# A delta-rule attention with two expert layers: two buffers for r's second layout, whole-row moves of y, each unit's second product reordered, and the weights' low word multiplied on DVE

## The chip, the cores and the metric

One core of a Trainium2 chip runs the whole program. The metric is the device time of one execution in microseconds (us); lower is better. PE is the matmul engine (PEld its weight loads), DVE, ACT and POOL are the vector, scalar and GpSimd engines, and SP is the engine whose queue issues all the DMAs of this kernel.

## The reference

Three stages follow each other. Every array of the attention has 4 batches, 8 heads, 768 steps and 40 channels; the 3072 tokens have 320 features.

```python
# attention, per batch and head, state 40x40
for t in range(768):
    y[t] = r[t] @ state
    Sa = state @ a[t]
    state = state * w[t] - outer(Sa, b[t]) + outer(v[t], k[t])
# first expert layer: one expert, d_ff 2048; its weights come as float64
x = relu(x @ w_in) ** 2 @ w_out
# second expert layer: four experts, d_ff 1024, mixed by normalised probabilities
out = sum(p[:, e:e + 1] * (relu(x @ w1[e]) @ w2[e]) for e in range(4))
```

## The kernel before

**Tiling.** The time axis is cut into 12 chunks of 64, and each chunk into two steps `s` (24 steps, `attention`), one for each half of the batches (`hb`). Two consecutive steps make one block `k` of 256 tokens (12 blocks). Within a chunk the recurrence is solved in closed form: scans and reciprocals of the decay on DVE (L371, L391), scaling on POOL (L395, L403), products on PE, and a triangular inverse (`invert`, one for each block) of 31 rounds of a multiplication and a subtraction on DVE (L691, L694). The recurrence between chunks runs through `f_mm` (L507), which reads the state and `rf`, a second layout of r that `load_rf` (L337) brings in with a DMA of its own. The tile `rf` has one buffer: the planner's line L357 lets the load of one step start when `f` of the step before has read it.

**From attention to the first layer.** `ys_y` (L632, POOL) leaves a block's output in the tile `y`, as [128, half, head, time]. `to_x1` (L807) turns it into the features-by-tokens tile `xr` with 12 DMAs of 40, 24 or 8 rows each; in `y`, one row of one head is four pieces of 64 numbers that don't lie side by side. `split` takes `xr` apart into a high part `xh` (L818, ACT) and the rest `xl` (L821, DVE), so that PE can multiply in its rounded fp32 format with the accuracy of fp32.

**First expert layer.** A block has 16 units (`moe1_l1`, `moe1_sq`, `moe1_l2`). A unit is 8 matmuls of 256 columns (`ffn1`, L197); ReLU (L753), square (L755) and the rounded copy `gh` (L758) on ACT; the remainder `gl` on POOL (L761); and `ffn2`, 6 matmuls of 320 columns into two accumulators in the order gh, gh, gl for the first and gh, gh, gl for the second (L202 to L204).

**Weights.** The first expert layer's weights come as float64 in 48 slices (`weights`). For each slice ACT takes the absolute value of the high word (L249) and scales the low word by 2^-52 (L250); DVE clamps, shifts, sets the sign and cuts out the power of two (L252, L253, L255, L257); POOL multiplies the low word by that power (L259); ACT rounds (L233); PE adds up the remainder (L237, L239, L240); ACT stores it (L243, L245).

**Second expert layer.** After the last block, 384 units of the same two functions run with nothing else on PE. Each unit's `ffn2` stands one unit behind its `ffn1`.

**What sets the order.** All work up to the units of the last block is entered in a planner, `Schedule`, with an engine, a due time (`DUE`, `LEAD`), the operations it depends on, a planned duration, and the buffers it needs. `run` simulates the engines and writes each engine's instructions in the order that comes out, the SP queue's too; at run time each engine takes its instructions in that fixed order. `PORT` (L62, used at L101 and L120) names operations of DVE and POOL that the simulation does not let overlap. The planned durations are constants in the calls of `op`; a wrong one changes the order and nothing else.

Of the kernel before, what the change touches and what calls it, by code (L numbers as in the profile page):

```python
# [29 lines left out]

E_MIN = 2.0 ** -15
# [9 lines left out]
DUE = dict(block=59.25, step=[-2.0, 3.5, -2.5, 0.3, 0.0], invert=[5.4, -11.9, -40.2], ffn=-2.4, w=[-85.9, 2.32], on_pe=48)  # L41
# [6 lines left out]
class Schedule:  # L48
# [13 lines left out]
    PORT = dict(DVE=("P", "t", "x1l"), POOL=("sq", "scale_a", "kb", "yq", "yf", "w_mul", "w_add"))  # L62
# [74 lines left out]
def tile_delta_rule_moe(  # L137
# [76 lines left out]
    def weights(n, t0):  # L214
# [4 lines left out]
        on_pe = n < DUE["on_pe"]  # L219
# [15 lines left out]
        def rest():  # L235
            v["pw"] = ps1.tile([128, 256], F32, tag="l1", name=f"pw{n}")[:, 0:k]
            pe.matmul(v["pw"], ident, v["m"], start=True, stop=False)  # L237
            if on_pe:
                pe.matmul(v["pw"], ident, v["f"], start=False, stop=False)  # L239
            pe.matmul(v["pw"], idneg, wt[i][:, c0:c1], start=False, stop=True)  # L240

        def low():
# [7 lines left out]
        op(o("w_lo"), "ACT", lambda: act.mul(v["lo"], v["li"], 2.0 ** -52), t0, [o("w_ld")], 0.29)  # L250
# [8 lines left out]
        op(o("w_mul"), "POOL", lambda: pool.tensor_tensor(v["f"], v["lo"], v["f"], ALU.mult),  # L259
           t0 + 2, [o("w_pow"), o("w_lo")] + [("tt", 0)] * (n >= 12), 0.65)  # L260
        if not on_pe:
            op(o("w_add"), "POOL", lambda: pool.tensor_tensor(v["m"], v["m"], v["f"], ALU.add), t0 + 2, [o("w_mul")], 0.65)
        op(o("w_hi"), "ACT", hi, t0 + 2, [o("w_sign" if on_pe else "w_add"), ("w_hi", n - 1)], 0.27)
        op(o("w_pe"), "PE", rest, t0 + 3, [o("w_hi"), o("w_mul")], 0.98 if on_pe else 0.55, alloc=[("l1", 2, [o("w_low")])])
# [25 lines left out]
    def attention(s, tt):  # L290
# [44 lines left out]
        def load_rf():  # L335
            d["rf"] = ap1.tile([128, 4, 128], F32, tag="rf", name=f"rf{s}")
# [20 lines left out]
        op(o("ld_rf"), "SP", load_rf, tt - LEAD["ld_xv"], [], prev=("ld_rf", s - 1), lat=2.7, alloc=[("rf", 1, [o("f")])])  # L357
# [172 lines left out]
        for h in range(2):  # L530
            for j in range(2):
                op(o("a_xv", h, j), "ACT", lambda h=h, j=j: a_xv(h, j), tt - LEAD["vm"], [o("ld_xv"), o("scale_a")], 0.29)
                op(o("s_xv", h, j), "ACT", lambda h=h, j=j: s_xv(h, j), tt - LEAD["f"], [o("ld_xv"), ("yf", s - 2, h)], 0.22)
# [4 lines left out]
        for h in range(2):  # L538
            for j in range(2):
                op(o("vmm", h, j), "DVE", lambda h=h, j=j: vm_mask(h, j), tt - LEAD["vm"] + h, [o("vm"), o("ld_xv")], 0.6)  # L540
# [3 lines left out]
            for j in range(2):  # L544
                op(o("fx", h, j), "ACT", lambda h=h, j=j: f_xv(h, j), tt - LEAD["f"] + h, [o("f"), o("ld_xv")], 0.26)
# [4 lines left out]
            op(o("xc", h), "ACT", lambda h=h: x_copy(h), tt - LEAD["x"] + h, [o("x", h)], 0.4)  # L550
# [31 lines left out]
        for i in range(2):  # L582
            op(o("mt", i), "DVE", lambda i=i: merge1(i), tt - LEAD["merge"], td_in + txo, 0.34)
        op(o("merge1", 1), "PE", lambda: merge1(2), tt - LEAD["merge"], td_in + both("mc") + [("merge1", s - 1, 1)], 0.68,
           alloc=at_bank("", ("y2",)) + [("y2", 1, [o("merge2")])])
        op(o("y2"), "ACT", lambda: merge1(3), tt - LEAD["merge"], [o("merge1", 1)], 0.53)
        op(o("merge2"), "PE", lambda: merge2(0), tt - LEAD["merge"] + 2, td_in + [o("y2")], 0.68, alloc=at_bank("", ("t2",)))
        op(o("t2"), "ACT", lambda: merge2(1), tt - LEAD["merge"] + 2, [o("merge2")], 0.53)
# [55 lines left out]
        for h in range(2):  # L644
# [7 lines left out]
            if not last:  # L652
# [5 lines left out]
               alloc=[] if hb + h else [("y", 1, [("tx1", k, i) for i in range(12)])])  # L658
# [414 lines left out]
```

## Time and profile before

| what | us |
|---|---|
| median of three runs | 1611.57 (1609.05 to 1613.45) |
| the profiled execution, its own time | 1609.46 |
| its span, first to last instruction | 1607.7 |
| PE busy in the span | 1444.4 (90%) |
| DVE, ACT, POOL busy | 835.0, 752.1, 379.6 |

The span is 1.8 us under the execution's own time, and that execution is 2.1 us under the median. PE's share alone doesn't say where time can be had: attention and the first expert layer fill the span up to about 865 us, the last block's units that up to 897 us, and the second expert layer the rest.

### The profile page before, as it was taken

What the parts mean: (1) busy time and instruction counts of PE and PEld (TensorE: products, weight loads), DVE (VectorE), ACT (ScalarE), POOL (GpSimd) and SP (SyncE); (2) the same over time, 40 slices, a digit from 0 to 9 for tenths busy, and PEclk for the clock granted to TensorE, in tenths of its full rate; (3) what the DMA queues carried; (4) which work ended last, traced back from release to release, by engine and by line L of the source; (5) the groups of instructions that cost most, each with busy time, mean ns of one, the idle gap of its engine ahead of it and who ended that gap; (6) DMA issues with size and microseconds to landing.
All of it is one profiled execution on the core that took longest, in us unless ns stands there. A gap on an engine that the chain in (4) does not pass through costs nothing.

```text
span 1607.7 us, 39782 instructions
## 1 busy us (share of the span) xinstructions
PE 1444.4 (90%) x16336; PEld 1354.8 (84%) x16336; DVE 835.0 (52%) x1944; ACT 752.1 (47%) x1991; POOL 379.6 (24%) x539
## 2 busy tenths in 40 slices
PE   5487989889779798887988999999999999999999
PEld 4366777878668687776888999999999999999998
DVE  8888767685675857759542233323333333332332
ACT  6477676566565656656666433322222222222221
POOL 5345443443324343343324200000000000000000
PEclk9798999999899898999999999999999999999999
DMA  7454243342333423243214111100000000000000
GB/s 235 117 144 144 68 126 76 105 122 56 110 73 103 118 56 110 65 117 92 61 32 125 46 50 46 56 1 28 28 19 1 19 10 1 1 7 20 26 26 25
DMA packets 147733, 107.18 MB, mean 67 GB/s; under 512 B 114400, under 2 KB 122080, under 8 KB 147552
## 3 DMA queue, kind: packets, MB, share of 16 engines
q1 hardware_dynamic: 147552, 104.64, 23.2%
q8 instruction: 129, 2.11, 0.5%
q14 instruction: 52, 0.43, 0.1%
HBM read 85.34 MB, written 14.55 MB: 62 GB/s over the span
## 4 chain that ended last, share of the span: by engine, by line
PE 48%; SPq 1%; DVE 1%; DMA 1%; ACT 0%; issue 0%; POOL 0%; DVEq 0%; ACTq 0%
PE z L197 22%; PE pz L204 7%; PE pz L202 7%; PE pz L203 7%; PE h L197 2%; SPq L807 1%; PE py L204 1%; PE py L202 0%; PE ptr L922 0%; PE py L203 0%; DVE xv L601 0%; DMA mu<-md 0%; PE pys L609 0%; DMA td<-mu 0%; PE ptx L597 0%
## 5 line engine op out<-in xcount | busy, mean ns | idle before, releaser
L969 DVE SCALAR_TENSOR_TENSOR zl<-z,zh 128x256 fp32r<-128x256 f32 x384 | 163.0, 425 | 476.4 <-ACT zh L968 476.4
L968 ACT ACTIVATE zh<-z 128x256 fp32r<-128x256 f32 x384 | 147.1, 383 | 510.5 <-PE z L197 510.5
L197 PE MATMUL z<-x2h,w 128*128 128x256 f32 x1920 | 380.8, 282 | 0.0
L197 PE MATMUL z<-x2l,w 128*128 128x256 f32 x1152 | 320.4, 278 | 0.0
L197 PEld LDWEIGHTS z<-x2h,w 128*128 128x128 f32 x1920 | 306.2, 188 | 0.0
L203 PE MATMUL pz<-w,zh 128*128 128x320 f32 x768 | 237.3, 309 | 0.0
L204 PE MATMUL pz<-w,zl 128*128 128x320 f32 x768 | 237.0, 309 | 0.0
L202 PE MATMUL pz<-w,zh 128*128 128x320 f32 x768 | 236.8, 308 | 0.0
L761 POOL TENSOR_TENSOR gl<-r,gh 128x256 fp32r<-128x256 f32 x192 | 144.7, 755 | 320.6 <-ACT gh L758 251.3
L197 PE MATMUL h<-xh,w 128*128 128x256 f32 x960 | 213.2, 304 | 6.2 <-ACT xh L818 6.1
L197 PEld LDWEIGHTS z<-x2l,w 128*128 128x128 f32 x1152 | 216.8, 188 | 0.0
L197 PEld LDWEIGHTS h<-xh,w 128*128 128x128 f32 x960 | 168.6, 206 | 11.3 <-ACT xh L818 6.8
L197 PE MATMUL h<-xl,w 128*128 128x256 f32 x576 | 171.9, 299 | 1.6 <-DVE xl L821 1.6
L691 DVE TENSOR_TENSOR tmp<-mu,t 128x126 f32<-128x126 f32 (+22 forms) x372 | 128.9, 347 | 46.7 <-DMA mu<-md 35.3
L753 ACT ACTIVATE r<-h 128x256 f32<-128x256 f32 x192 | 73.4, 382 | 153.6 <-PE h L197 130.4
L204 PEld LDWEIGHTS pz<-w,zl 128*128 128x128 f32 x768 | 144.3, 188 | 0.1
L202 PEld LDWEIGHTS pz<-w,zh 128*128 128x128 f32 x768 | 144.3, 188 | 0.0
L203 PEld LDWEIGHTS pz<-w,zh 128*128 128x128 f32 x768 | 144.2, 188 | 0.0
L204 PE MATMUL py<-w,gl 128*128 128x320 f32 x384 | 125.8, 328 | 19.1 <-POOL gl L761 17.9
L202 PE MATMUL py<-w,gh 128*128 128x320 f32 x384 | 128.0, 333 | 9.5 <-ACT gh L758 9.1
L185 POOL TENSOR_TENSOR w<-raw,w 64x128 fp32r<-64x128 f32 x32 | 31.6, 988 | 441.5 <-ACT w L183 405.9
L694 DVE TENSOR_TENSOR t<-t,tmp 128x126 f32<-128x126 f32 (+22 forms) x372 | 123.0, 331 | 9.0
(105 smaller groups left out, 2491.4 us busy)
## 6 DMA issues: line engine op xcount, KB each, us to landing
in<-kba SPq DMA_DIRECT2D x24, 768.0 KB
raw<-wf SPq DMA_DIRECT2D x32, 352.0 KB
raw<-wm SPq DMA_DIRECT2D x32, 234.0 KB
wd<-w SPq DMA_DIRECT2D x24, 264.0 KB
r<-rv SPq DMA_DIRECT2D x24, 256.0 KB
v<-rv SPq DMA_DIRECT2D x24, 256.0 KB
rf<-rv SPq DMA_DIRECT2D x24, 256.0 KB
mu<-md SPq DMA_DIRECT2D x24, 256.0 KB
```

The costliest lines, as they stand in the source:

```text
L185: pool.tensor_tensor(t[64:128, 576:704], raw[64:128, 576:704], t[64:128, 576:704].bitcast(F32), ALU.subtract)
L197: pe.matmul(ps, a, b, start=n == 0, stop=n == len(mm) - 1)
L202: pe.matmul(pys[tt], gh[:, sl], t[:, 256:576], start=first, stop=False)
L203: pe.matmul(pys[tt], gh[:, sl], t[:, 960:1280], start=False, stop=False)
L204: pe.matmul(pys[tt], gl[:, sl], t[:, 256:576], start=False, stop=last)
L691: dve.tensor_tensor(v["tmp"], a, b, ALU.mult)
L694: dve.tensor_tensor(c, c, v["tmp"], ALU.subtract)
L753: act.activation(g["r"], g["ps"], AF.Relu)
L761: pool.tensor_tensor(g["gl"], g["r"], g["gh"].bitcast(F32), ALU.subtract)
L807: sp.dma_start(v["raw"][r0:r0 + e1 - e0, kc].rearrange("p (a b x) -> p a b x", a=2, b=2), src)
L968: act.activation(gh, ps, AF.Relu)
L969: dve.scalar_tensor_tensor(gl, ps, 0.0, gh.bitcast(F32), ALU.max, ALU.subtract)
```

## The change

1. `rf` gets two buffers; its load waits for `f` of the step before last.
2. `y` is laid out as [128, head, half and half of the heads, time], so that the four pieces of one head lie side by side, and each of the 12 moves reads one run of 256 numbers in a row.
3. `ffn2` runs the four matmuls with gh first and the two with gl last. In the first expert layer, ACT writes `gh` as the square of the ReLU directly; the unrounded square comes after it, in place.
4. For the weights, ACT's scaling of the low word and POOL's multiplication go; DVE does both in one operation. The condition that held slices from the 13th on back until the first inverse was turned goes with POOL's operation.
5. The planner's `PORT` names DVE's operations of the weights; `w_mul` and `w_add` leave POOL's list. Twelve planned durations are raised (by 0.02 to 0.24). The setting `on_pe` was 48, all slices, so what it chose stays.

```diff
-DUE = dict(block=59.25, ..., w=[-85.9, 2.32], on_pe=48)
+DUE = dict(block=59.25, ..., w=[-85.9, 2.32])
...
-    PORT = dict(DVE=("P", "t", "x1l"), POOL=("sq", "scale_a", "kb", "yq", "yf", "w_mul", "w_add"))
+    PORT = dict(
+        DVE=("P", "t", "x1l", "w_clamp", "w_shift", "w_sign", "w_pow", "w_mul"),
+        POOL=("sq", "scale_a", "kb", "yq", "yf"),
+    )
...
             pe.matmul(pys[tt], gh[:, sl], t[:, 256:576], start=first, stop=False)
             pe.matmul(pys[tt], gh[:, sl], t[:, 960:1280], start=False, stop=False)
+        for tt in range(2):
+            sl = slice(tt * 128, tt * 128 + 128)
             pe.matmul(pys[tt], gl[:, sl], t[:, 256:576], start=False, stop=last)
...
-        op(o("w_lo"), "ACT", lambda: act.mul(v["lo"], v["li"], 2.0 ** -52), t0, [o("w_ld")], 0.29)
...
-        op(o("w_mul"), "POOL", lambda: pool.tensor_tensor(v["f"], v["lo"], v["f"], ALU.mult),
-           t0 + 2, [o("w_pow"), o("w_lo")] + [("tt", 0)] * (n >= 12), 0.65)
+        op(o("w_mul"), "DVE", lambda: dve.scalar_tensor_tensor(
+            v["f"], v["li"], 2.0 ** -52, v["f"], ALU.mult, ALU.mult), t0 + 1, [o("w_pow")], 0.32)
...
-            d["rf"] = ap1.tile([128, 4, 128], F32, tag="rf", name=f"rf{s}")
+            d["rf"] = ap2.tile([128, 4, 128], F32, tag="rf", name=f"rf{s}")
...
-        op(o("ld_rf"), ..., alloc=[("rf", 1, [o("f")])])
+        op(o("ld_rf"), ..., alloc=[("rf", 2, [o("f")])])
...
-                d["y"] = ap1.tile([128, 2, 8, 64], F32, tag="y", name=f"y{s}")
+                d["y"] = ap1.tile([128, 4, 4, 64], F32, tag="y", name=f"y{s}")
-            pool.tensor_tensor(st[2 * k]["y"][:, hb, hs], d["t", h][:, :, 0:64], d["q"][:, hs], ALU.mult)
+            pool.tensor_tensor(st[2 * k]["y"][:, :, 2 * hb + h], d["t", h][:, :, 0:64], d["q"][:, hs], ALU.mult)
...
         elif i == 1:
+            g["gh"] = fp.tile([128, 256], F32R, tag="gh", name=f"gh{k}_{f}", bufs=3)
+            act.activation(g["gh"], g["r"], AF.Square)
+        elif i == 2:
             act.activation(g["r"], g["r"], AF.Square)
-        elif i == 2:
-            g["gh"] = fp.tile([128, 256], F32R, tag="gh", name=f"gh{k}_{f}", bufs=3)
-            act.copy(g["gh"], g["r"])
...
-            src = y[64 * (hd % 2) + e0:64 * (hd % 2) + e1, :, hd // 2::4]
-            sp.dma_start(v["raw"][r0:r0 + e1 - e0, kc].rearrange("p (a b x) -> p a b x", a=2, b=2), src)
+            src = y[64 * (hd % 2) + e0:64 * (hd % 2) + e1, hd // 2].rearrange("q a x -> q (a x)")
+            sp.dma_start(v["raw"][r0:r0 + e1 - e0, kc], src)
```

## Rows read from the trace of the kernel before

**Rows 1.** Busy time by stretch: us, then PE, PEld, DVE, ACT, POOL, granted clock, DMA.
```profile
0.00:132.00 132.00, 78.56 (x1243) 62.36 (x1243) 112.23 (x299) 81.32 (x247) 55.78 (x77) 0.87 0.58 174
...
410.00:480.00 70.00, 58.20 (x888) 51.51 (x888) 45.21 (x105) 42.21 (x111) 25.63 (x38) 0.89 0.36 92
...
897.00:1607.70 710.70, 706.78 (x5446) 706.40 (x5444) 225.62 (x502) 185.06 (x456) 25.05 (x25) 1.00 0.07 23
```
**Rows 2.** PE in order of time near 475 us: start, us, operation [idle before <-releaser].
```profile
467.39 0.69 PE L507 MATMUL pf<-rf,SS 64*64 64x64 f32 x32
...
477.35 1.12 PE L493 MATMUL pk<-cs,in 128*128 128x128 f32 x4 [2.08 <-ACT m L440]
481.97 1.32 PE L507 MATMUL pf<-rf,SS 64*64 64x64 f32 x32 [3.51 <-DMA rf<-rv]
```
**Rows 3.** The SP queue in order of time, same stretch.
```profile
467.47 10.67 SPq L807 DMA_DIRECT2D xr<-y  x12
478.24 0.44 SPq L781 DMA_DIRECT2D y1d<-y  x1
478.78 0.36 SPq L337 DMA_DIRECT2D rf<-rv  x1
```
**Rows 4.** DVE in order of time, same stretch.
```profile
480.49 0.96 DVE L821 TENSOR_TENSOR xl<-xr,xh 128x768 fp32r<-128x768 f32 x1 [0.69 <-ACT xh L818]
```
**Rows 5.** Waits up to 865 us: who waited for whom, total us, times, longest.
```profile
PE pf L507 <- DMA rf<-rv: 28.8, 7, 10.6
...
PE py L204 <- POOL gl L761: 17.7, 36, 1.7
...
PE pw L239 <- POOL raw L259: 17.5, 9, 8.1
...
PE h L197 <- ACT xh L818: 6.1, 3, 4.0
```
**Rows 6.** Lines 807, 348 and 818 alone: duration ns min/median/max, first and last start.
```profile
L807 SPq DMA_DIRECT2D xr<-y x144: 721/778/1687, 112.6 to 860.5; - x144
...
L348 SPq DMA_DIRECT2D xv<-vn x24: 533/554/684, 5.0 to 797.1; - x24
...
L818 ACT CAST xh<-xr x12: 831/831/855, 124.5 to 862.8; 128x768 fp32r<-128x768 f32 x12
```
**Rows 7.** The chain that ended last, from 844 us: start, us, what.
```profile
850.05 0.74 POOL y L632
...
851.51 0.84 SPq L807
...
864.72 5.07 PE h L197 x23
...
870.67 0.95 PE h L197 x8
```
**Rows 8.** Lines 252 and 255 alone, as rows 6.
```profile
L252 DVE TENSOR_SCALAR raw<-raw x48: 219/276/1585, 9.4 to 173.6; 128x234 f32<-128x234 f32 x32, 128x236 f32<-128x236 f32 x16
...
L255 DVE SCALAR_TENSOR_TENSOR raw<-raw x48: 333/397/919, 11.6 to 174.5; 128x234 uint32<-128x234 uint32 x32, 128x236 uint32<-128x236 uint32 x16
```
**Rows 9.** Groups by line and shape up to 860 us: busy us, mean ns | idle before.
```profile
L259 POOL TENSOR_TENSOR raw<-raw 128x234 f32<-128x234 f32 x32 | 24.0, 753 | 35.4 <-DVE tmp L691 10.2 <-DVE raw L257 7.1 <-PE pw L240 5.1
...
L252 DVE TENSOR_SCALAR raw<-raw 128x234 f32<-128x234 f32 x32 | 13.9, 434 | 10.8 <-ACT raw L249 10.6
...
L250 ACT ACTIVATE raw<-raw 128x234 f32<-128x234 uint32 x32 | 13.1, 409 | 0.0
```
**Rows 10.** POOL in order of time, 44 to 90 us.
```profile
76.86 2.72 POOL L259 TENSOR_TENSOR raw<-raw 128x236 f32<-128x236 f32 x5
```
**Rows 11.** PE in order of time in the second expert layer, 1200 to 1204 us.
```profile
1201.44 0.31 PE L202 MATMUL pz<-w,zh 128*128 128x320 f32 x1
...
1201.74 0.31 PE L204 MATMUL pz<-w,zl 128*128 128x320 f32 x1
1201.88 0.31 PE L202 MATMUL pz<-w,zh 128*128 128x320 f32 x1
```

More of the change, by code (lines that the diff above doesn't have):

```diff
@@ L28 @@
 C_U, C_NEG, C_ID, C_ONE, C_END = 0, 64, 168, 296, 560
+MOVES = []
+for _kc in range(2):
+    MOVES += [(40 * _i, _kc, 3 * _kc + _i, 0, 40) for _i in range(3)]
+    MOVES.append((120, _kc, 6, 8 * _kc, 8 * _kc + 8))
+for _r in (0, 64):
+    MOVES += [(_r, 2, 6, 16, 40), (_r + 24, 2, 7, 0, 40)]
 E_MIN = 2.0 ** -15
@@ L36, in sub @@
     return AP(base.tensor, base.offset, [list(base.ap[0])] + dims)
-DUE = dict(block=59.25, step=[-2.0, 3.5, -2.5, 0.3, 0.0], invert=[5.4, -11.9, -40.2], ffn=-2.4, w=[-85.9, 2.32], on_pe=48)
+DUE = dict(block=59.25, step=[-2.0, 3.5, -2.5, 0.3, 0.0], invert=[5.4, -11.9, -40.2], ffn=-2.4, w=[-85.9, 2.32])
 LEAD = dict(
@@ L237, in rest @@
             pe.matmul(v["pw"], ident, v["m"], start=True, stop=False)
-            if on_pe:
-                pe.matmul(v["pw"], ident, v["f"], start=False, stop=False)
+            pe.matmul(v["pw"], ident, v["f"], start=False, stop=False)
             pe.matmul(v["pw"], idneg, wt[i][:, c0:c1], start=False, stop=True)
@@ L258, in weights @@
             v["fi"], v["mi"], 0xFF800000, None, ALU.bitwise_and), t0 + 1, [o("w_sign")], 0.19)
-        op(o("w_mul"), "POOL", lambda: pool.tensor_tensor(v["f"], v["lo"], v["f"], ALU.mult),
-           t0 + 2, [o("w_pow"), o("w_lo")] + [("tt", 0)] * (n >= 12), 0.65)
[L261 to L264, printed above, removed]
+        op(o("w_mul"), "DVE", lambda: dve.scalar_tensor_tensor(
+            v["f"], v["li"], 2.0 ** -52, v["f"], ALU.mult, ALU.mult), t0 + 1, [o("w_pow")], 0.32)
+        op(o("w_hi"), "ACT", hi, t0 + 2, [o("w_sign"), ("w_hi", n - 1)], 0.29)
+        op(o("w_pe"), "PE", rest, t0 + 3, [o("w_hi"), o("w_mul")], 0.98, alloc=[("l1", 2, [o("w_low")])])
         op(o("w_low"), "ACT", low, t0 + 4, [o("w_pe")], 0.3)
@@ L544, in attention @@
             for j in range(2):
-                op(o("fx", h, j), "ACT", lambda h=h, j=j: f_xv(h, j), tt - LEAD["f"] + h, [o("f"), o("ld_xv")], 0.26)
+                op(o("fx", h, j), "ACT", lambda h=h, j=j: f_xv(h, j), tt - LEAD["f"] + h, [o("f"), o("ld_xv")], 0.37)
             op(o("fc", h), "ACT", lambda h=h: f_copy(h), tt - LEAD["f"] + h, [o("f"), ("ya", s - 2, h)], 0.26)
@@ L582, in attention @@
         for i in range(2):
-            op(o("mt", i), "DVE", lambda i=i: merge1(i), tt - LEAD["merge"], td_in + txo, 0.34)
+            op(o("mt", i), "DVE", lambda i=i: merge1(i), tt - LEAD["merge"], td_in + txo, 0.45)
         op(o("merge1", 1), "PE", lambda: merge1(2), tt - LEAD["merge"], td_in + both("mc") + [("merge1", s - 1, 1)], 0.68,
            alloc=at_bank("", ("y2",)) + [("y2", 1, [o("merge2")])])
-        op(o("y2"), "ACT", lambda: merge1(3), tt - LEAD["merge"], [o("merge1", 1)], 0.53)
+        op(o("y2"), "ACT", lambda: merge1(3), tt - LEAD["merge"], [o("merge1", 1)], 0.76)
         op(o("merge2"), "PE", lambda: merge2(0), tt - LEAD["merge"] + 2, td_in + [o("y2")], 0.68, alloc=at_bank("", ("t2",)))
-        op(o("t2"), "ACT", lambda: merge2(1), tt - LEAD["merge"] + 2, [o("merge2")], 0.53)
+        op(o("t2"), "ACT", lambda: merge2(1), tt - LEAD["merge"] + 2, [o("merge2")], 0.76)
         def tx_mm():
@@ L657, in attention @@
             op(o("yq", h), "POOL", lambda h=h: ys_y(h), tt - LEAD["yq"] + h, [o("ya", h), o("scale_a")] + ([("yq", 2 * k, 0)] if hb + h else []), 0.69,
-               alloc=[] if hb + h else [("y", 1, [("tx1", k, i) for i in range(12)])])
+               alloc=[] if hb + h else [("y", 1, [("tx1", k, i) for i in range(len(MOVES))])])
         if not last:
@@ L824, in split @@
                     sp.dma_start(dbg[k], v["raw"])
[L826 to L831 removed]
         ys = [("yq", 2 * k + b, h) for b in range(2) for h in range(2)]
         done = [("x1h", k), ("x1l", k)]
[L834 removed]
+        for i in range(len(MOVES)):
             op(("tx1", k, i), "SP", lambda i=i: to_x1(i), tt - LEAD["x1"], ys + ([] if i else [("x1l", k - 1)]), 0.65, prev=("tx1", k, 0) if i else None,
                alloc=[] if i else [("ws", 5, done)])
[L837 removed]
+        moved = [("tx1", k, i) for i in range(len(MOVES))]
         end = [("l1", k, NF1 - 1)]
@@ L1017, in _arrays @@
         vn[:, n, :, 4:] = v[:, 4:, n].transpose(0, 2, 1, 3)
-    hd = [(h, e) for h in (0, 1, 2) for e in range(D)] + [(6, e) for e in range(8)]
-    hd += [(h, e) for h in (3, 4, 5) for e in range(D)] + [(6, e) for e in range(8, 16)]
-    hd += [(6, e) for e in range(16, 40)] + [(7, e) for e in range(D)]
+    hd = [(h, e) for _, _, h, e0, e1 in MOVES[:10] for e in range(e0, e1)]
     feat = np.array([h * D + e for h, e in hd])
```

23 lines of the change are left out of this document (7 added, 16 removed).

## The prediction

> **What bounds the kernel now.** The busy times by stretch come first. From 897 us on, PE is busy for 706.8 of 710.7 us at a granted clock of 1.00 [rows 1]: the second expert layer is a plain queue of matmuls, and only what changes their number or pace changes it. What can be won lies before. In a middle block (410 to 480 us) PE is busy for 58.2 of 70 us and the other engines for 45 or less, at a mean clock of 0.89: no engine is full, and PE, the fullest, loses its time in waits and at the lower clock. In the first 132 us it is DVE that is full, 112.2 of 132.
>
> Next, PE in order of time around the end of a block. It waits 2.08 us for ACT's copy of m, and 3.51 us for the DMA that loads `rf` [rows 2]. The SP queue shows why that DMA is late: the step before freed the one buffer at 468.1 (467.39 + 0.69), but the twelve moves of y began at 467.47 and held the queue for 10.67 us; the load of rf went out at 478.78 [rows 2, 3]. The table of waits puts 28.8 us of PE on this load, in 7 waits. The longest, 10.6, is the kernel's first load; that leaves 18.2 in six later ones [rows 5]. The matmuls behind such a stop run at half pace: the same 32 matmuls take 1.32 us instead of 0.69 [rows 2].
>
> The chain of waits from 844 us shows the moves themselves. In the last block y is ready at 850.8, the twelve issues take until about 861.4, and h begins at 864.72 [rows 7]. Blocks follow each other at (862.8 - 124.5) / 11 = 67.1 us [rows 6].
>
> **The change part by part.**
>
> *Two buffers for rf.* The load now waits for a read that lies a whole step back, so SP can issue it ahead of the twelve moves; nothing new queues behind it. In the block of rows 2, `f` could start at about 478.2, behind pk. Six waits go: **18.2 us**. What is late next: h needs xl, which ends at 480.49 + 0.96 = 481.45 [rows 4], while `f` now ends at 481.97 + 1.32 = 483.29 and h starts there. Alone, then, the two buffers give only 1.8 per block; the rest hangs on the next part.
>
> *Moves of one run per row.* The twelve stay twelve, each with a source of two dimensions instead of four. No row shows a move inside SBUF with such a source. Bounds for one issue: 0.36, a plain load [rows 3], and 0.78, as now [rows 6]; a load with a three-dimensional target takes 0.55 [rows 6]. I take 0.44, the store of a plain SBUF tile [rows 3], since it has the same kind of source. Then 12 x (0.78 - 0.44) = 4.1 us are saved before xh, and xl ends at about 477.4, before `f` would: the 18.2 can be kept. Where PE waits for xh itself, 6.1 us in three blocks, the longest 4.0 [rows 5], the 4.1 covers each wait.
>
> *The clock.* After the stop in rows 2 the 32 matmuls cost 0.63 too much. In the last block 23 matmuls of h took 5.07 us, 0.22 each, against 0.95 / 8 = 0.119 later [rows 7]: that is the lower of the two levels, 1.2 against 2.4 GHz. Two units (16 matmuls) at that pace cost 1.6 us, with the 0.63 some 2.2 per block, 13.4 in six. The wait for m stays, so the clock may still fall: I take half, **6.7**, bounds 0 and 13.4. For the last block likewise half of 5.07 - 23 x 0.119 = 2.3; with the 6.1 that makes **7.3**.
>
> *Order in the second product.* PE waits for gl 36 times, 17.7 us in all [rows 5]. Two more matmuls (0.15 each [rows 11]) now run before the wait, so each shrinks by at most 0.29: 10.6 us in all, fewer where the wait was shorter. ACT still runs three operations before gl, so gl comes no earlier. I take **6**, bounds 0 and 10.6. In the second expert layer gl is never late (3.9 us of idle in 710.7 [rows 1]), so nothing is won there. The order changes accumulator four times a unit instead of twice. A step into another accumulator takes 0.14 (1201.74 to 1201.88), two steps within one 0.30 (1201.44 to 1201.74) [rows 11]: switching costs nothing, and the term is 0. The Trainium skill speaks against this edit: "TensorE: Matmul & The Clock Gate", section "A second HAM failure mode: psum-queue depth-cycling", tells of a kernel that cycled through accumulator banks and whose clock swung between its levels. Here PE already changes banks in every unit and the clock is 1.00 [rows 1]; by that rule the time would be that of the last rival.
>
> *The low word on DVE.* ACT loses 48 operations of 0.41 and POOL 48 of 0.75 [rows 9]; neither is full. DVE gains 48. The nearest shape is L255, two tensor inputs with the same strides: median 0.397 [rows 8], so 48 x 0.397 = 19.1 us in the stretch in which DVE is full. Against that, POOL held DVE up: L252 takes 0.276 in the median, but up to 1.585 [rows 8] and 0.434 in the mean [rows 9], 0.158 x 48 = 7.6 us for this one of four lines. The 19.8 us that DVE idles in the first 132 can hold the remaining 11.5. PE waited 17.5 us for POOL's product [rows 5], and five products that waited for the first inverse ran together at 76.86 [rows 10]; that condition goes. Bounds: a loss of 19.1, if nothing comes back, and a gain of 17.5 + 7.6 = 25.1. The two nearly cancel on DVE; of PE's 17.5 I take a quarter: a gain of **4**.
>
> *The planner.* New durations and the port rewrite every engine's order up to 865 us, which no row shows. One wait like the 2.08 of rows 2 more or less in each of nine later blocks is 19 us either way; I take 0.
>
> **Sum.** 18.2 + 6.7 + 7.3 + 6 + 4 = 42.2. The profiled execution took 1609.5, so 1567.3; the median lies 2.1 above it, so **1569**.
>
> **The rivals.**
>
> *The stop moves instead of going.* If an issue keeps 0.78, h waits for xl: 1.8 per block (483.29 to 481.45), 10.8 in six, with 6 for gl and 4 for the weights 20.8: 1611.6 - 20.8 = 1591. If the new order leaves the rf load behind the moves, the first two terms go and 17.3 remains: 1594. For it: moves of 8 to 40 rows have a shortest of 0.72 and a median of 0.78 [rows 6], so it is not the rows that set the price, and perhaps not the pieces either. Against: the plain store behind them costs 0.44 [rows 3].
>
> *The new order removes more.* PE idles 11.8 us of 70 [rows 1], of which I take away less than half. Another 2.08 in nine blocks: about 1550.
>
> *The weights come too late (the slower side).* Place: the first 180 us. DVE alone now carries five operations a slice, between the 62 of each inverse. If it pushes the weights back, the first blocks' units cannot fill PE's gaps, and they end up behind the attention, where nothing overlaps them. Price: a block's 16 units of 0.95 + 6 x 0.15 = 1.85 us, 29.6 per block of lag. It decides once the lag eats the other terms, 42.2 - 4 = 38.2: from 1.3 blocks on. At two blocks: 1611.6 - 38.2 + 59.2 = 1633. Against it: DVE's busy time in the first 132 us barely grows by the count above.
>
> *The order gives everything back,* the terms eaten by new waits: about 1610.
>
> *The clock falls in the second expert layer.* At 1.2 GHz a unit of 1.85 costs another 1.7 or so (0.22 against 0.119 a matmul). From 38.2 / 1.7 = 23 of 384 units on, the kernel is slower than my forecast by all it had won; at one unit in ten, 1569 + 65 = 1634.
>
> **How the numbers follow.** Forecast 0.58, more removed 0.12, the stop moves 0.17, no change 0.04, late weights 0.08, clock 0.01. A difference of about 0.3% (5 us) is what a measurement of this kernel can tell from none. Faster 0.58 + 0.12 + 0.17 = 0.87, same 0.04, slower 0.09. The range runs from 1543 (the order's 19 and the other half of the clock's 13.4 on top of the forecast) to 1600, which holds the first rival at both its prices with a few us for the weights; what lies above and below is under 2 in 10.
>
> **What would show it.** In the profile after: L807's median near 0.44; the moves of a block under 6 us; the load of rf ahead of them and no wait of PE on it after the first; xh then ready before `f` ends, and the clock in middle blocks above 0.95; the waits for gl fewer or shorter by 0.3; no line for ACT's or POOL's part of the weights, the DVE line near 0.4 and L252's mean nearer its median; the second expert layer still about 711 us. I am wrong if L807 stays near 0.78, if PE waits for xh or for another load in rf's place, if the weights' last L255 starts later than now (174.5 us), or if blocks still follow at over 65 us.

## The result, and the profile after

The changed kernel takes **1570.09 us** in the median of four runs (1568.11 to 1590.19), the kernel before 1611.51 beside it; the ratio is **0.9755, with the interval 0.9716 to 0.9793**. The profiled run took 1568.11, its span is 1566.3, 41.4 less than before. The kernels before that ran beside the experiments on other chips had medians from 1611.5 to 1616.8; so kernels are compared below by their ratios, and by microseconds only within a trace.

The number forecast was 1569. The steps to it were mostly wrong, as the rest of this document shows.

First the busy time by stretch (columns as in [rows 1]): the first stretch, a block in the middle, five blocks from the split of x in the fifth to that in the tenth, and the second expert layer.

```profile
0.00:123.00 123.00, 84.65 (x1221) 66.69 (x1221) 106.83 (x328) 71.70 (x216) 30.75 (x46) 0.83 0.59 169
398.00:460.00 62.00, 53.68 (x888) 48.87 (x888) 46.12 (x104) 41.73 (x111) 25.75 (x38) 0.97 0.37 101
398.25:713.34 315.09, 275.04 (x4440) 248.55 (x4440) 236.05 (x518) 208.12 (x551) 128.58 (x190) 0.96 0.37 100
856.00:1566.30 710.30, 706.14 (x5442) 705.81 (x5440) 225.55 (x502) 184.88 (x456) 25.08 (x25) 1.00 0.07 23
```

The second expert layer is as long as it was, 710.3 against 710.7 us [rows 1]. The same five blocks before:

```profile
410.24:750.35 340.11, 285.11 (x4440) 251.95 (x4440) 227.15 (x515) 209.06 (x550) 129.01 (x190) 0.92 0.35 92
```

They are 25.0 us shorter: PE, with the same 4440 matmuls, is busy for 10.1 us less and idle for 14.9 less (55.0 to 40.1). Up to the second block's split of x 18.3 us are won (215.1 to 196.8), of which 7.0 are left at the third's (279.2 to 272.2); then it is 37.0 up to the tenth's and 40.5 up to the last one's (862.8 to 822.3). Behind that, almost nothing.

Now the end of a block, on PE and then on the SP queue (start, us, operation [idle before <-releaser]).

```profile
396.74 0.68 PE L515 MATMUL pf<-rf,SS 64*64 64x64 f32 x28 [1.00 <-ACT m L448]
399.30 0.63 PE L501 MATMUL pk<-cs,in 128*128 128x128 f32 x4 [1.88 <-DVE xv L493]
...
401.04 0.58 PE L208 MATMUL h<-xl,w 128*128 128x256 f32 x1 [0.99 <-DVE xl L829]
```
```profile
387.46 9.15 SPq L815 DMA_DIRECT2D xr<-y  x12
396.72 0.42 SPq L345 DMA_DIRECT2D rf<-rv  x1
397.26 0.36 SPq L330 DMA_DIRECT2D in<-kba  x1
397.71 3.37 SPq L454 DMA_DIRECT2D md<-mb  x4
```

Against [rows 2, 3]: `f` runs at full pace and no longer waits for `rf`. But the load of `rf` still stands behind the twelve moves, not ahead of them; it serves a later `f`. And the load of `in` (the inputs that POOL scales) now leaves 0.65 us behind the moves. Before, it left 4.3 us behind them (they ended at 478.14):

```profile
482.42 0.43 SPq L322 DMA_DIRECT2D in<-kba  x1
```

PE's largest waits up to 825 us, to hold against [rows 5]:

```profile
PE pys L617 <- DVE xv L609: 21.2, 33, 1.9
PE pk L501 <- DVE xv L493: 15.4, 8, 2.3
PE py L217 <- POOL gl L769: 13.7, 15, 1.8
PE pf L515 <- DMA rf<-rv: 13.0, 1, 13.0
PE h L208 <- ACT xh L826: 12.9, 6, 5.5
```

Of the seven waits for `rf` only the kernel's first is left. The waits for gl fell from 36 to 15, by 4.0 us; those for xh doubled, from 6.1 to 12.9. The two largest have grown most: 36.6 us for DVE's `xv`, against 12.7 before, where the same two waits were

```profile
PE pys L609 <- DVE xv L601: 9.6, 28, 0.9
...
PE pk L493 <- DVE xv L485: 3.1, 7, 1.4
```

Around the end of the block shown, DVE works without a gap, and `xv` stands in its order between operations of the inverse. Last, the lines alone that answer to [rows 6] and [rows 8], with the new DVE operation L269 (duration ns min/median/max, first and last start):

```profile
L815 SPq DMA_DIRECT2D xr<-y x144: 658/716/1830, 111.7 to 819.8; - x144
L826 ACT CAST xh<-xr x12: 831/832/833, 123.2 to 822.3; 128x768 fp32r<-128x768 f32 x12
...
L265 DVE SCALAR_TENSOR_TENSOR raw<-raw x48: 375/393/1466, 12.8 to 167.0; 128x234 uint32<-128x234 uint32 x32, 128x236 uint32<-128x236 uint32 x16
L269 DVE SCALAR_TENSOR_TENSOR raw<-raw x48: 331/394/927, 13.8 to 169.7; 128x234 f32<-128x234 uint32 x32, 128x236 f32<-128x236 uint32 x16
```

A move's issue fell from 0.778 to 0.716 only. The new operation costs what L255 cost before, and the last slice of weights comes 7.5 us earlier (L265 at 167.0, its like before at 174.5).

### The profile page after: what moved, and what is told of

Same layout as the page of the kernel before. It is cut to its first block, busy times and chain, and to the rows that moved or that the text cites. A ratio compares the mean times of both kernels' runs of the same rounds, so it can differ in the third digit from the quotient of the medians.

```text
span 1566.3 us, 39677 instructions
## 1 busy us (share of the span) xinstructions
PE 1438.9 (92%) x16336; PEld 1360.4 (87%) x16336; DVE 841.7 (54%) x1992; ACT 739.1 (47%) x1943; POOL 345.9 (22%) x491
## 4 chain that ended last, share of the span: by engine, by line
PE 56%; DVE 8%; DMA 5%; SPq 4%; issue 2%; POOL 1%; ACT 1%; DVEq 0%; ACTq 0%; POOLq 0%
PE z L208 23%; PE pz L214 7%; PE pz L217 7%; PE pz L213 7%; PE h L208 5%; SPq L815 4%; DVE xv L609 2%; DVE tmp L699 2%; DVE t L702 2%; PE py L217 1%; DMA mu<-md 1%; PE py L213 1%; PE py L214 1%; DMA td<-mu 1%; PE pys L617 1%
## 5 line engine op out<-in xcount | busy, mean ns | idle before, releaser
L208 PE MATMUL z<-x2l,w 128*128 128x256 f32 x1152 | 320.4, 278 | 0.0
L214 PE MATMUL pz<-w,zh 128*128 128x320 f32 x768 | 231.3, 309 | 0.0
L213 PE MATMUL pz<-w,zh 128*128 128x320 f32 x768 | 230.6, 308 | 0.0
L208 PE MATMUL h<-xh,w 128*128 128x256 f32 x960 | 210.6, 302 | 13.0 <-ACT xh L826 12.9
L217 PE MATMUL pz<-w,zl 128*128 128x320 f32 x768 | 175.0, 309 | 0.0
L699 DVE TENSOR_TENSOR tmp<-mu,t 128x126 f32<-128x126 f32 (+22 forms) x372 | 133.3, 358 | 49.2 <-DMA mu<-md 41.6
L702 DVE TENSOR_TENSOR t<-t,tmp 128x126 f32<-128x126 f32 (+22 forms) x372 | 128.4, 345 | 8.9
L217 PEld LDWEIGHTS pz<-w,zl 128*128 128x128 f32 x768 | 128.4, 188 | 0.0
L208 PEld LDWEIGHTS h<-xl,w 128*128 128x128 f32 x576 | 117.3, 204 | 7.1 <-DVE xl L829 7.1
```

Of the source, the lines that this page charges most:

```text
L208: pe.matmul(ps, a, b, start=n == 0, stop=n == len(mm) - 1)
L699: dve.tensor_tensor(v["tmp"], a, b, ALU.mult)
L702: dve.tensor_tensor(c, c, v["tmp"], ALU.subtract)
```

## The experiments

Twelve kernels ran. "after" means an edit to the changed kernel, "before" one to the old kernel. The table gives each one's median, its ratio to the kernel before with the interval, and the five blocks from the fifth split of x to the tenth in its trace (length; PE busy; PE idle, the difference; granted clock). These four columns are of one execution for each kernel, the one that was profiled.

| kernel | us | ratio [interval] | five blocks | busy | idle | clock |
|---|---|---|---|---|---|---|
| before | 1611.5 | 1 | 340.1 | 285.1 | 55.0 | 0.92 |
| after | 1570.1 | 0.9755 [0.9716, 0.9793] | 315.1 | 275.0 | 40.1 | 0.96 |
| after, one rf | 1564.8 | 0.9682 [0.9651, 0.9712] | 310.9 | 276.7 | 34.2 | 0.97 |
| after, old y | 1578.0 | 0.9761 [0.9720, 0.9802] | 320.4 | 281.2 | 39.2 | 0.94 |
| after, old second product | 1573.6 | 0.9732 [0.9700, 0.9764] | 317.2 | 277.9 | 39.3 | 0.95 |
| after, weights as before | 1590.0 | 0.9838 [0.9808, 0.9868] | 317.9 | 278.7 | 39.1 | 0.95 |
| after, old durations | 1596.6 | 0.9896 [0.9866, 0.9927] | 340.8 | 286.8 | 54.0 | 0.92 |
| after, old DVE port list | 1594.0 | 0.9882 [0.9831, 0.9933] | 337.6 | 290.9 | 46.7 | 0.91 |
| after, six DMAs more | 1620.8 | one run | 339.0 | 283.5 | 55.6 | 0.91 |
| before, two rf | 1626.9 | 1.0088 [1.0054, 1.0122] | 354.2 | 294.7 | 59.6 | 0.90 |
| before, two rf, `in` first | 1598.1 | 0.9902 [0.9870, 0.9934] | 326.7 | 280.0 | 46.8 | 0.94 |
| before, planner alone | 1590.2 | 0.9850 [0.9804, 0.9897] | 318.4 | 283.2 | 35.2 | 0.95 |
| before, rf pinned | 1612.2 | 0.9990 [0.9972, 1.0009] | 337.3 | 288.8 | 48.5 | 0.92 |
| after, one rf, y through DRAM | 1556.7 | 0.9635 [0.9602, 0.9667] | 317.4 | 278.5 | 38.9 | 0.94 |

### One part of the change undone

**One buffer for rf.** The planner rewrites the order for it.

```diff
-            d["rf"] = ap2.tile([128, 4, 128], F32, tag="rf", name=f"rf{s}")
+            d["rf"] = ap1.tile([128, 4, 128], F32, tag="rf", name=f"rf{s}")
...
-        op(o("ld_rf"), ..., alloc=[("rf", 2, [o("f")])])
+        op(o("ld_rf"), ..., alloc=[("rf", 1, [o("f")])])
```

> The changed kernel with rf back at one buffer, everything else of the change kept. Theory (the rf load behind the moves of y was the stop that the change took away): PE waits for the rf load again, about 3 us in each middle block, the clock falls behind it, blocks follow each other some 3 us later, and the time rises by 20 to 30 us to 1590 to 1600. Rival (the planner's new durations and port made the gain, whichever load they put where): the time stays within 6 us of 1570 and PE waits for rf less than 6 us in all after the first load.

Measured: 0.9682, below the changed kernel's 0.9755 (the medians differ by 5.3 us, the ratios by 0.7%, and the intervals only just don't touch). The first theory, on which the forecast stood, fails: with one buffer the stop on `rf` does not come back, since only two waits for it are in the trace (18.1 us, of which 13.0 is the first load's).

**The old layout of y**, with its four-dimensional source for the moves, in the order of the changed kernel.

```diff
-                d["y"] = ap1.tile([128, 4, 4, 64], F32, tag="y", name=f"y{s}")
+                d["y"] = ap1.tile([128, 2, 8, 64], F32, tag="y", name=f"y{s}")
...
-            src = y[64 * (hd % 2) + e0:64 * (hd % 2) + e1, hd // 2].rearrange("q a x -> q (a x)")
-            sp.dma_start(v["raw"][r0:r0 + e1 - e0, kc], src)
+            src = y[64 * (hd % 2) + e0:64 * (hd % 2) + e1, :, hd // 2::4]
+            sp.dma_start(v["raw"][r0:r0 + e1 - e0, kc].rearrange("p (a b x) -> p a b x", a=2, b=2), src)
```

> The changed kernel with y in its old layout, so that each move of y has a four-dimensional source again; the planner sees no difference, so the order of all engines stays. What the profile of the changed kernel shows (an issue of a move costs 0.716 us against 0.778 before): issues at about 0.778, a block's twelve moves 0.75 us longer, and the time up by 0 to 6 us. Rival (as the prediction had it, the layout is worth 4 us per block on the way to the next block's h): the time up by 15 us or more.

Measured: 0.9761, not to be told from the changed kernel. The moves alone:

```profile
L815 SPq DMA_DIRECT2D xr<-y x144: 721/778/973, 112.9 to 832.1; - x144
```

The layout is worth 0.06 per issue, 0.7 a block; the five blocks are 1.1 longer each in this trace.

**The old order of the second product**, with `gh` copied from the square.

```diff
             pe.matmul(pys[tt], gh[:, sl], t[:, 960:1280], start=False, stop=False)
-        for tt in range(2):
-            sl = slice(tt * 128, tt * 128 + 128)
             pe.matmul(pys[tt], gl[:, sl], t[:, 256:576], start=False, stop=last)
...
-            g["gh"] = fp.tile([128, 256], F32R, tag="gh", name=f"gh{k}_{f}", bufs=3)
-            act.activation(g["gh"], g["r"], AF.Square)
-        elif i == 2:
             act.activation(g["r"], g["r"], AF.Square)
+        elif i == 2:
+            g["gh"] = fp.tile([128, 256], F32R, tag="gh", name=f"gh{k}_{f}", bufs=3)
+            act.copy(g["gh"], g["r"])
```

> The changed kernel with the second product of a unit in its old order (gh, gh, gl, twice) and gh made by the copy after the square, as before; planned durations stay. Theory (two matmuls ahead of the wait for gl are worth up to 0.29 us at each late gl): PE's waits for gl and gh rise from 13.7 us to 20 to 26, and the time rises by 5 to 10 us. Rival (PE's time there is taken up by other waits of the same blocks): within 3 us of 1570.

Measured: 0.9732, the same as the changed kernel. PE's waits for gl, up to 830 us:

```profile
PE py L215 <- POOL gl L767: 22.1, 26, 3.5
```

They rise by 8.4 us (13.7 to 22.1), those for gh by 3.1 (0.7 to 3.8), and the time doesn't follow: in the five blocks PE idles 39.3 us, against 40.1 in the changed kernel, so other waits are shorter by as much.

**The weights on ACT and POOL again**, with the condition on the first inverse.

```diff
-        op(o("w_mul"), "DVE", lambda: dve.scalar_tensor_tensor(
-            v["f"], v["li"], 2.0 ** -52, v["f"], ALU.mult, ALU.mult), t0 + 1, [o("w_pow")], 0.32)
+        op(o("w_lo"), "ACT", lambda: act.mul(v["lo"], v["li"], 2.0 ** -52), t0, [o("w_ld")], 0.29)
+        op(o("w_mul"), "POOL", lambda: pool.tensor_tensor(v["f"], v["lo"], v["f"], ALU.mult),
+           t0 + 2, [o("w_pow"), o("w_lo")] + [("tt", 0)] * (n >= 12), 0.65)
```

> The changed kernel with the weights' low word scaled on ACT and multiplied on POOL as before, the condition on the first inverse included, and POOL's list of the port naming it; the rest of the change kept. Theory (POOL's multiplication and its condition held the weights and DVE up): the second block's x split starts 5 to 15 us later than the 196.8 us of the changed kernel, and the time is up by 4 to 12 us. Rival (DVE pays for the multiplication in the stretch in which it is full): the first block's split starts earlier than 123 us and the time falls by 4 us or more.

Measured: 0.9838, 0.83% or 13 us above the changed kernel (the medians differ by 20). Here the place is plain. The stretch up to 123 us:

```profile
0.00:123.00 123.00, 76.28 (x1129) 60.29 (x1130) 99.17 (x278) 71.20 (x214) 46.31 (x72) 0.82 0.55 161
```

By 123 us PE has done 1129 matmuls, 1221 with the weights on DVE. The second block's split starts at 209.69 against 196.76, and that difference, 12.9, stays to the end, where it is 16.2 (the last split at 838.4 against 822.3). PE's wait for POOL's product, 17.5 us before [rows 5], is 12.6 in this kernel and gone in the changed one, where waits for the new DVE operation come to about 4. The operation and the condition on the first inverse came back together, so how the 13 us are shared between them is open.

### The planner

**Old durations** and, in another kernel, the **old DVE port list**; no operation of the changed kernel differs, only the order. (The change raises nine durations, by 0.02 to 0.23, not twelve: the eight that are put back here, and `w_hi` of the weights from 0.27 to 0.29, which stays raised.)

```diff
-    PORT = dict(DVE=("P", "t", "x1l", "w_clamp", "w_shift", "w_sign", "w_pow", "w_mul"), ...
+    PORT = dict(DVE=("P", "t", "x1l"), ...
```

> The changed kernel with the eight planned durations that the change raised for a_xv, s_xv, vmm, fx, xc, mt, y2 and t2 put back; only the planner's order can differ. Theory (the parts themselves make the gain): within 8 us of 1570, either way. Rival (the truer durations make a good part of it): 1580 or more, with new waits of PE in middle blocks.

> The changed kernel with the planner's port naming only the three operations of DVE that it named before; DVE's operations of the weights are left out of it, and they still run on DVE. Only the order of the first 180 us or so can differ. Theory (DVE's own multiplication gives the early gain, not the order): the second block's x split starts within 4 us of 196.8 us and the time stays within 5 us of 1570. Rival (the modelled port gives it): the second split starts 8 us or more later, time 1576 or more.

Measured: 0.9896 and 0.9882; each undone alone costs 1.3 to 1.4%, and the five blocks go back to about the old length (340.8 and 337.6 us, 340.1 before). The port list names operations that end by about 170 us; through the planner it changes the order hundreds of us later. With the old durations PE's waits in these blocks are led by

```profile
PE py L217 <- POOL gl L769: 24.3, 12, 4.1
PE pk L501 <- ACT m L448: 12.1, 10, 2.1
```

**The planner alone**, on the kernel before: eight of the new durations and the port list for the operations that exist there, nothing else.

```diff
-    PORT = dict(DVE=("P", "t", "x1l"), POOL=...)
+    PORT = dict(DVE=("P", "t", "x1l", "w_clamp", "w_shift", "w_sign", "w_pow"), POOL=...)
...
-                op(o("a_xv", h, j), "ACT", ..., 0.29)
+                op(o("a_xv", h, j), "ACT", ..., 0.41)
...
-        op(o("y2"), "ACT", lambda: merge1(3), tt - LEAD["merge"], [o("merge1", 1)], 0.53)
+        op(o("y2"), "ACT", lambda: merge1(3), tt - LEAD["merge"], [o("merge1", 1)], 0.76)
```

> The kernel before with the planner's numbers alone changed: the eight raised durations, and the port naming the four operations of DVE on the weights (POOL's multiplication stays where it was, in POOL's list). No operation of the program changes. Theory (the order makes most of the gain): blocks from 68 to 65 us or less, time 1580 to 1597. Rival (the order only fits together with the cheaper weights and the other edits): 1605 or more.

Measured: 0.9850, **24 us** without one changed operation, with one buffer for `rf` and the old moves. On PE, at the end of a block:

```profile
474.56 0.66 PE L493 MATMUL pk<-cs,in 128*128 128x128 f32 x4 [0.52 <-ACT m L440]
477.52 0.38 PE L197 MATMUL h<-xh,w 128*128 128x256 f32 x1 [2.30 <-ACT xh L818]
...
482.00 0.69 PE L507 MATMUL pf<-rf,SS 64*64 64x64 f32 x32
```

The order itself has taken the stop on `rf` away: `f` now stands behind the first two units' h, 6.8 us after its load's issue at 475.23, and needs no second buffer. What PE waits for in these five blocks:

```profile
PE h L197 <- ACT xh L818: 11.4, 5, 2.4
...
PE pk L493 <- ACT m L440: 2.3, 5, 0.5
```

The wait for m, which the forecast left in place, went from 11.9 us in the same blocks before to 2.3, and the 13.9 for `rf` are gone; of the stop, 11.4 are now a wait for xh, for which PE had not waited in these blocks.

### Two buffers for rf on the kernel before

**As planned.** The edit is the first one of this section, turned round, on the kernel before; the planner knows of it.

> The kernel before with two buffers for rf and nothing else of the change. Theory (the rf load behind the moves is the main stop): PE's waits for rf fall from 18.2 us behind the first load to under 4, the blocks' distance from 67 to 63 to 65, time 1578 to 1592. Rival (the stop passes to the split of x, which ends 1.8 us before h starts): 1595 to 1602. Second rival (without the new durations the planner wins nothing): 1608 or more.

Measured: 1.0088, **14 us slower**. Behind the first load the waits for `rf` are gone, and PE waits 25.7 us for gl in five blocks instead of 9.2. SP and then POOL behind the moves of one block:

```profile
477.35 9.85 SPq L807 DMA_DIRECT2D xr<-y  x12
...
488.31 3.00 SPq L446 DMA_DIRECT2D md<-mb  x4
...
493.75 0.44 SPq L322 DMA_DIRECT2D in<-kba  x1
```
```profile
499.60 1.17 POOL L403 TENSOR_TENSOR in<-in,P 128x512 f32<-128x512 f32 x1 [3.19 <-DMA in<-kba]
...
501.94 1.83 POOL L761 TENSOR_TENSOR gl<-r,gh 128x256 fp32r<-128x256 f32 x2
```

The second load of `in` goes out 6.5 us behind the moves; POOL, which works in order, stands at the scaling of `in` for 3.19 us, and two gl queue behind that. PE's next matmul with gl had waited 4.24 us when it began at 503.12. In the five blocks POOL's waits for `in` add up to 15.1 us, against 1.8 before:

```profile
POOL in L403 <- DMA in<-kba: 15.1, 5, 3.8
```

**The same with `in` first.** In that kernel's SP queue alone, the store of the first layer's result (`y1d`) and the four stores of md, which stood before loads of `in`, go behind them, and so behind the other loads in between; every other engine keeps its order.

```diff
-        for _, _, fn in sorted(order, key=lambda x: x[:2]):
-            fn()
+        order.sort(key=lambda x: x[:2])
+        late = [x[0] for x in order if x[3][0] == "ld_in"]
+        when = lambda x: (min([a + 0.01 for a in late if 0 < a - x[0] < 7], default=x[0]) if x[3][0] in ("mo", "y1o") else x[0])
+        when2 = lambda x: when((when(x), x[1], x[2], x[3]))
+        for x in sorted(order, key=lambda x: (when2(x), x[1])):
+            x[2]()
```

> The kernel before with two buffers for rf, and one more change in the SP queue alone: the store of the first layer's result (y1d) and the stores of m that stand up to 7 us ahead of a load of the in tile go behind it, so that in a middle block five DMAs change places with two loads; PE, DVE, ACT and POOL keep their order. Theory (with rf out of the way, the late load of in holds POOL's scaling, gl stands behind that on POOL, and PE waits for gl): PE's wait for gl in a middle block falls from 5.2 to under 2.5 us, blocks follow each other by 66 to 68.5 us instead of 70.8, time 1596 to 1612 against 1627. Rival (the load isn't what decides, the matmuls' order is): within 6 us of 1627.

Measured: 0.9902 against 1.0088, **30 us** by the ratios (29 by the medians), for five DMAs a block that changed places. The queue now:

```profile
478.62 0.39 SPq L326 DMA_DIRECT2D in<-kba  x1
479.10 1.14 SPq L785 DMA_DIRECT2D y1d<-y  x1
480.33 4.28 SPq L450 DMA_DIRECT2D md<-mb  x4
```

POOL's waits for `in` are gone from the five blocks, and PE's for gl fall to 12.0. So for this order the chain from the SP queue through `in` and POOL to gl is shown, not only argued. A late `in` by itself need not cost: in the changed kernel POOL waits 21.9 us for it in the five blocks, more than the 15.1 above, and PE waits only 8.0 for gl. With `in` first, the two buffers are 16 us ahead of the kernel before; what `in` first gives with one buffer did not run.

**rf alone, everything else pinned.** The kernel before in its own order; `rf` has two tiles of which the planner knows nothing, and only the one load that stood behind the moves goes ahead of them.

```diff
...
+        first = {x[3][1]: x[0] for x in reversed(order) if x[3][0] == "tx1"}
+        loads = [x for x in order if x[3][0] == "ld_rf"]
+        early = {}
+        for t0 in first.values():
+            for x in loads:
+                if t0 < x[0] < t0 + 14:
+                    early[x[3]] = t0 - 0.01
+                    break
+        for x in sorted(order, key=lambda x: (early.get(x[3], x[0]), x[1])):
+            x[2]()
...
```

> The kernel before with two buffers for rf, the planner left unaware of the second one, and in the SP queue the one load of rf that stood behind each block's twelve moves put ahead of them; every other DMA and all instructions of PE, DVE, ACT and POOL keep their order. This is the first term of the prediction by itself. As the prediction had it (PE's stop goes, h is held by xl at most): PE's waits for rf gone behind the first load, 11 to 25 us gained, 1588 to 1602 on a chip where the kernel before takes 1612. Theory by now (the load of in, further back in the same queue, becomes what PE waits for through POOL and gl): the wait for gl in a middle block rises from 2.0 us by 1 to 3, blocks shrink by less than 2 us, and the time falls by 12 us at most. If the time rises by 5 us or more, as with the planner's own order, neither holds.

Measured, over ten runs: 0.9990, between 0.28% faster and 0.09% slower. The waits for `rf` (13.9 us in five blocks) are gone. These are there now:

```profile
PE pk L502 <- ACT m L449: 12.1, 10, 2.1
PE py L213 <- POOL gl L770: 12.1, 16, 2.3
...
PE h L206 <- ACT xh L827: 5.1, 5, 1.5
...
PE h L206 <- DVE xl L830: 2.2, 5, 0.6
```

The wait for m is as it was (11.9 before). What stands in the place of `rf` is h's wait for xh and xl, 7.3 us where there was none, and 2.9 more for gl (9.2 before). POOL's waits for `in` rose as well, from 1.8 to 8.2. So most of the stop went to the split of x, the next thing that the prediction had named, and less to gl. At the end of one block, on PE:

```profile
479.79 0.66 PE L502 MATMUL pk<-cs,in 128*128 128x128 f32 x4 [2.08 <-ACT m L449]
480.38 0.69 PE L516 MATMUL pf<-rf,SS 64*64 64x64 f32 x32
482.61 0.58 PE L206 MATMUL h<-xh,w 128*128 128x256 f32 x1 [1.54 <-ACT xh L827]
```

PE idles 6.5 us less in the five blocks, but is busy for 3.7 more at the same clock, 0.92: 2.9 us are left. `f` runs at full pace, 0.69, but the matmuls behind the new stop don't, and for longer than before: at 489.60 one with gh takes 0.47, where the same one had taken 0.31.

### The moves

**Six more DMAs behind each block's moves**, of other shapes, to price an issue and to see whether the queue is on the path.

```diff
...
+            if i == len(MOVES) - 1:
+                sp.dma_start(probe[0:40, 0], y[0:40, 0, 0, 0:32])
+                sp.dma_start(probe[0:48, 1], y[0:48, 0, 0, 0:32])
+                sp.dma_start(probe[0:64, 2], y[0:64, 0, 0, 0:32])
+                sp.dma_start(probe[:, 3], y[:, 0, 0, 0:32])
+                sp.dma_start(pdram[0, 0:40], y[0:40, 0, 0, 0:32])
+                sp.dma_start(pdram[1], y[0:64, 0, 0, 0:32])
```

> The changed kernel with six more DMAs behind each block's twelve moves, each out of y with one run of 32 numbers per row: to a spare SBUF tile with 40, 48, 64 and 128 rows, and to DRAM with 40 and 64 rows. It measures the price of an issue by itself; the time is of no interest. Theory (the number of rows sets it: where it isn't a multiple of 16, the issue takes another branch): 40 rows about 0.7 us, to SBUF and to DRAM alike; 48, 64 and 128 rows about 0.35 to 0.45. Rival (a move inside SBUF is dear): the four into SBUF about 0.7, the two to DRAM about 0.4. Second rival (fewer than 128 rows are dear): only the one of 128 rows is cheap.

Measured, in the order of the diff (ns min/median/max of the issue; SBUF to SBUF with 40, 48, 64 and 128 rows, then SBUF to DRAM with 40 and 64):

```profile
L819 SPq DMA_DIRECT2D probe<-y x12: 707/707/707, 119.9 to 871.6; - x12
L820 SPq DMA_DIRECT2D probe<-y x12: 551/557/882, 120.6 to 872.4; - x12
...
L822 SPq DMA_DIRECT2D probe<-y x12: 579/592/596, 121.9 to 873.6; - x12
L823 SPq DMA_DIRECT2D pdram<-y x12: 521/522/525, 122.5 to 874.2; - x12
L824 SPq DMA_DIRECT2D pdram<-y x12: 475/481/1507, 123.1 to 874.8; - x12
```

In this order of the six the target counts (0.707 to SBUF, 0.522 to DRAM, both with 40 rows), and so do the rows (0.707 with 40, 0.557 with 48); the order was not varied. The bytes hardly do: the moves, also of 40 rows for the most part, cost 0.716 with eight times the numbers per row. The six take 3.5 us of the queue a block (their medians, 0.592 for the third among them), and a block grows by 4.8 (63.0 to 67.8, one execution each): in the changed kernel, what stands on SP behind the moves is on the path.

**y through DRAM.** Two stores and four loads in place of the twelve moves, on the kernel with one rf buffer; the features come in natural order, and the weights are laid out for that.

```diff
...
+            sp.dma_start(v["raw"][r0:r1, kc], v["xd"][f0:f0 + r1 - r0])
+
+        def to_xd(p):
+            if p == 0:
+                v["xd"] = dram.tile([320, 256], F32, tag="xd", name=f"xd{k}")
             y = st[2 * k]["y"]
-            r0, kc, hd, e0, e1 = MOVES[i]
-            src = y[64 * (hd % 2) + e0:64 * (hd % 2) + e1, hd // 2].rearrange("q a x -> q (a x)")
-            sp.dma_start(v["raw"][r0:r0 + e1 - e0, kc], src)
+            dst = v["xd"].rearrange("(a p e) x -> p e a x", a=4, p=2)[p]
+            sp.dma_start(dst, y[64 * p:64 * p + 40].rearrange("q b a x -> q b (a x)"))
...
```

> The changed kernel with one buffer for rf, and the twelve moves of y replaced by two stores to DRAM (40 rows each) and four loads from there (128, 128, 64 and 64 rows); the features of the first layer then stand in their natural order. Theory (what stands behind the moves in the SP queue is late by as long as they take, which the run with six more DMAs showed: 3.5 us more on SP made a block 4.8 us longer): the queue is held for 3 to 4 us of issues instead of 8.6, the loads behind it leave earlier, blocks at 57 to 60 us instead of 62, time 1525 to 1553 against 1564. Rival (the way through DRAM takes a second landing, so xh is later and PE waits for it as long as it gains elsewhere): 1558 or more, with a wait for xh of over 2 us per block.

Measured: 0.9635, the lowest ratio of all, though its interval overlaps that of one rf with moves. The queue in a block:

```profile
509.75 0.71 SPq L820 DMA_DIRECT2D xd<-y  x2
...
513.53 2.01 SPq L813 DMA_DIRECT2D xr<-xd  x4
```

The six issues take 2.7 us of SP instead of 9.1. The split of x starts 9.7 us after the first store in the median of the twelve blocks, where it started 10.6 us after the first move, although the loads leave some 3 us behind the stores. But the middle blocks do not get shorter than with one rf and moves (63.5 against 62.2 us each): the blocks of 57 to 60 us that were expected did not come, and neither did the rival's wait for xh. PE's waits in the five blocks, first with moves, then through DRAM:

```profile
PE h L208 <- ACT xh L826: 7.8, 5, 1.6
...
PE h L208 <- DVE xl L829: 4.7, 5, 1.0
```
```profile
PE pk L501 <- DVE xv L493: 9.0, 4, 3.4
```

The waits for the split went, and one for DVE's `xv` came that the other kernel hardly has (0.8 us in all). The planner's order differs too, so the cause is not isolated. More on SP behind the moves costs, as the six DMAs show; less of it gave nothing back in these blocks. Against that kernel the 8 us lie in the first blocks and in the last two.

## Why the prediction was right in its number and wrong in its steps

What each part is worth is best read along one line of kernels, each with the order that the planner writes for it: planner alone 0.9850; with rf's buffers, y's layout and the second product added 0.9838 (the kernel with the weights as before); with the weights' part 0.9755. So of 1611.6 us the planner gives 24, the three parts on which 38.2 us of the forecast rested together about 2, not to be told from nothing, and the weights 13. That the forecast came within 2 us is luck: errors in its sum cancelled.

- **Two buffers for rf, 18.2.** Alone, with all else pinned, 1.6 us (from a gain of 4.5 to a loss of 1.5); as the old planner orders it, a loss of 14. "What is late next: h needs xl" was right: pinned, h waits 7.3 us in five blocks for the split of x. The step that failed is "the 18.2 can be kept", which rested on moves at 0.44. Nor did "only 1.8 per block" come, but 0.6 (2.9 in five): "nothing new queues behind it" left out the loads of `in`, which the same queue holds behind the moves, with POOL and gl behind them, and the lower pace of PE behind the new stop was not counted. The rival "The stop moves instead of going" had the right mechanism for this part; that the time is not its 1591 is the planner's work.
- **The moves at 0.44.** They cost 0.716. The bound of 0.78 was close, the value taken was not: "since it has the same kind of source" looked at the source, and in the probe target and rows change the price. So a block's moves take 9.15 us instead of under 6, and the split of x starts 10.8 us behind the first move, where it started 11.6 behind it (medians of the twelve blocks): 0.8 sooner, not 4.1. The waits for xh, in the last block too (5.5 us against 4.0 [rows 5]), went up and not away. Of the **7.3** for xh and the last block nothing came: from the last split to the end 0.8 us are won.
- **The clock, 6.7.** In the five blocks PE's busy time fell by 10.1 us and the mean clock rose from 0.92 to 0.96, so the size was about right. The reason given is not borne out: with the stop on `rf` taken away by itself, the clock stayed at 0.92 and busy time rose, but a shorter stop for the split of x stood there instead. With the planner alone it is at 0.95; of the waits there, the one before pk shrank (11.9 to 2.3 us) and those for `rf` went, while those for xh grew. Which of them the clock answers to was not isolated.
- **The second product, 6.** The waits for gl fell by 4.0 from the kernel before, and rise by 8.4 when the order is undone; the time answers with nothing that the intervals can tell. The step that failed is taking a wait's length for time.
- **Its four changes of accumulator at no cost.** This was right: the second expert layer takes 710.3 us at a clock of 1.00. What the Trainium skill tells of cycling through accumulator banks ("TensorE: Matmul & The Clock Gate", section "A second HAM failure mode: psum-queue depth-cycling") does not show in this trace.
- **The weights, 4.** The mechanism, that POOL's product held the weights up, was right, and the size was off: 13 us. DVE's price was right too (0.394 against 0.397 an operation). What was mis-sized is "of PE's 17.5 I take a quarter": nearly all of that wait went, and between these two kernels the time won in the first blocks stays won. The 7.6 us by which POOL's multiplication was to hold up DVE go mostly with the order: L252's mean of 434 ns [rows 9] is 338 at its like in the new order with POOL still multiplying, 325 without, and 387 without but with the old port list.
- **The planner, 0 within 19.** It is the largest term, 24 us, beyond the bound. The forecast had the waits that went (2.08 us for m in each block [rows 2]) in its rows and called what the order would do with them unknown. Of the signs listed, the rf load ahead of the moves, L807 near 0.44 and xh before the end of `f` were wrong; blocks under 65 us, the clock above 0.95, one wait for rf and the second layer at 711 came true. Of the signs of being wrong two showed: L807's like at 0.716, much nearer to 0.78 than to 0.44, and PE's longer waits for xh.

**Open.** Why one buffer for rf is faster than two in the changed kernel: with it the whole order differs (PE idles 5.9 us less in the five blocks; its wait before pk for DVE's `xv`, 15.4 us in the changed kernel, is 0.8), and the buffer was not tried with that order pinned. Nor was it settled how durations and port list share the planner's 24 us; each one undone from the changed kernel costs 20 to 23 us, so they do not add.

## What to carry to other kernels

Before a wait is priced as won, read what ends next on every engine and in the whole in-order queue that its release goes through: here the split of x took the stop over and, in another order, a load of `in` with POOL behind it; in the changed kernel the waits for DVE's `xv` grew most. Where a planner writes the order, an edit's own worth shows only with the order pinned, and planned lengths corrected to the measured ones may be worth more than every edit. Six waits of 18 us in all can vanish and leave the time where it was, when something else is ready only little sooner.

## What the runs showed of the hardware

The price of issuing a small DMA on SP was not what had been expected: a move inside SBUF of 40 rows costs 0.71 us of the queue, with 48 rows 0.56, with 128 rows 0.59, and the same 40 rows to DRAM 0.52; a source of one run per row instead of four pieces saves only 0.06. Through DRAM twelve moves became six DMAs of 2.7 us in all. There the two stores, also of 40 rows, cost only 0.35 each in the median, so rows and target do not settle the price.
